# A fused attention and feed-forward kernel: the first matrix product by seven products of quarter blocks in place of eight

## Chip, core and metric

One core of a Trainium2 chip runs the whole kernel. The metric is the device time of one execution in microseconds. The engines are TensorE (PE, matrix products into PSUM), VectorE (DVE), ScalarE (ACT), GpSimd (POOL) and SyncE (SP), which here issues DMA transfers. PSUM has eight banks of 128 x 512 fp32.

## What is computed

```python
def phi(x):                                  # batch 8, heads 8, 576 tokens, 64 wide
    proj = x @ w_phi                         # 64 x 128
    proj = proj - max(abs(proj), axis=-1)
    return concatenate([exp(proj), exp(-proj)])
q_p, k_p = phi(q), phi(k)
kv, z = k_p.T @ v, sum(k_p)
x = (q_p @ kv) / (q_p @ z + 1e-6)            # 4608 tokens x 512
h = x @ w_in                                 # 512 x 2048
g = h * erf(softplus(h))
out = g @ w_out                              # 2048 x 512
```

All is fp32; the weights come as pairs of 32-bit words (they are doubles on the host). The kernel keeps fp32 accuracy in the two large products by splitting each operand into a high and a low fp16 half and adding three products: high x high, high x low, low x high.

## The kernel before

The class `Plan` (line 108) is a list scheduler written into the kernel. Every operation is entered with its engine, a cost in ns, what it reads and writes, and a place in the wanted order (`plan.pos` plus an offset). `Plan.run` (184) then walks through a planned time: at each step it takes the engine that can start earliest and on it the ready operation with the smallest place. A reader on TensorE is held back by `SLACK` ns behind its data. Where the plan sees TensorE without work for over 600 ns it puts filler matmuls on the tile `hot` (1026, called "fillers" below). The result is one fixed order per engine; at run time each engine goes through its order and waits on semaphores.

Attention goes through 72 groups of four tiles of 128 tokens (two heads at a time, a "pair"; four pairs make a batch entry). For each group `project` (517) makes the projections of q and k on TensorE, `front` (485 to 496) takes the maximum and subtracts it on VectorE, `k_piece` makes the exponentials on ScalarE, `t_piece` turns q's part (by TensorE for pairs below `PE_TURNED`, line 568, by a DMA transpose with two VectorE copies, 582 to 585, for the others), `kv_piece` and `n_tile` multiply (helper `columns`, line 401), and `normalise` (644 on) divides. Pairs below `HALVED` are projected in fp32, the others in fp16 halves, made by `halve` (507, 510). The divided tile goes to `xf`, is split into fp16 halves in `xt` (660 to 665), and `x_piece` (700 on) transposes it by DMA into x's tile.

The feed-forward part works on 18 blocks of 256 tokens, each in two halves of eight 128-column groups of w_in. `h_chunk` (803) makes two groups into one PSUM bank: per group, four slices of the 512 inputs by three products, each a pair of matmuls of 64 output rows and 256 columns (helper `mm`, line 391). ScalarE reads each bank out once (822). `erf_gate` (838) applies softplus, erf and the product, and splits the result into `gh` and `gl` (857, 858). `o_chunk` (886) multiplies these by w_out, three products of 512 columns each. All of w_in and w_out stands in SBUF as fp16 halves (`wih`, `wil`, `woh`, `wol`); `load_weight` (423) loads a piece of double words, builds fp32 from the bits in three VectorE steps (440 to 444), and splits it on ScalarE and VectorE (448).

The order of the work is: attention of the first batch entry, then feed-forward halves, with the rest of attention spread between them at a rate set by `BATCH_NS`, and a last stage of feed-forward alone.

Of the kernel before, what the change touches and what calls it, by code (L numbers as in the profile page):

```python
# [8 lines left out]
F32 = mybir.dt.float32  # L9
# [14 lines left out]
TB = 256  # L24
NBLK = NT // TB
GF = 8
NG = 2 * NBLK
HW = GF * TB // 2

SW_PHI = 16.0  # L30
SX = 256.0
SWI = 256.0
# [3 lines left out]
BATCH_NS = 25000.0  # L36
LEAD = 1.05
EARLY = 2 * NPAIR
PE_TURNED = 8
SPEED = {}  # L40
STAY2 = 9000.0
N1 = 7
TWO = 24
ATTN = 5
PH = 2
REST = 4
# [3 lines left out]
X_POOL = 0, 12  # L50
HL_POOL = 8, 16
LATE = 1500.0
FIRST = 4
GAP = 2
XS = 6
N0 = 6
W_EARLY = 7
# [4 lines left out]
BIASED = 0, 9  # L62
KV_ACT = 1, 8
XT_ACT = 0, 12
WRS = 3
GATE_OFF = 4000.0, 4500.0, 5500.0
W_FROM = 12
W_EACH = 7
W_MM = 14
W_OFF = 4000.0  # L70
# [5 lines left out]
STAY = 2500.0  # L76
HALVED = 2 * NPAIR
# [226 lines left out]
def favor_attention_moe(ctx: ExitStack, tc: tile.TileContext, qk, vp, wphi, w_in, w_out, out):  # L304
# [17 lines left out]
    plan.kind("ph", "bank", (("ph",), PH))  # L322
    plan.kind("po", "bank", (("po",), 2))
    plan.kind("pk", "bank", (("pk",), 1))
    plan.kind("pj", "bank", (ATT, 3), (("pj",), 3))
    plan.kind("pj2", "bank", (ATT, ATTN), (("pj2",), ATTN))
    plan.kind("nd", "bank", (ATT, 3), (("nd",), 2))
    plan.kind("nd2", "bank", (ATT, ATTN), (("nd2",), 2))
    plan.kind("p0", "bank", (("p0", "ph", "po", "pk", "pj", "nd"), 7))
# [8 lines left out]
    slots("big", 18, [P, HW], F32)  # L338
    plan.kind("x", "big", (("x",), XS))
    pd = ctx.enter_context(tc.tile_pool(name="pd", bufs=1, space=bass.MemoryType.DRAM))  # L340
    for i in range(2 * FIRST):
        plan.slot("part", f"part{i}", pd.tile([P, DM], F32, tag=f"part{i}", name=f"part{i}"))
    plan.kind("part", "part")
    plan.kind("hs", "big", (("hs",), 4))
    plan.kind("L", "big", (("L",), 4))
    plan.kind("wr", "big", (("wr",), WRS))
    slots("half", 4, [P, 512], F32)
    plan.kind("wf", "half", (("wf",), 2))
    plan.kind("osb", "half", (("osb",), 4))
    plan.kind("acc", "half", (("acc",), 2))  # L350
    whole("gh", 4, [P, HW], F16)
# [16 lines left out]
    whole("xf", 2, [P, 256], F32)  # L368
    whole("xt", 2, [P, 5, 4 * P], F16)
# [5 lines left out]
    const = {k: buf(k) for k in ("ident", "wphi", "w1", "w2", "wih", "wil", "woh", "wol")}  # L375
# [3 lines left out]
    wih, wil, woh, wol = (const[k] for k in ("wih", "wil", "woh", "wol"))  # L379
# [6 lines left out]
    def mm(cost, get, r, w, start, stop):  # L386
        def fn():
            o, a, b = get()
            for i in range(2):
                half = slice(i * D, (i + 1) * D)  # L390
                nc.tensor.matmul(o[half], a[:, half], b, start=start, stop=stop)  # L391

        return op(PE, cost, fn, r=r, w=w, done=cost + 201, mode=COLS)
# [19 lines left out]
    wq = [*range(8), *range(16, 24), *range(8, 16), *range(24, 32)]  # L413
    loaded = set()

    def want(i):
        while i not in loaded:
            load_weight()

    def load_weight():  # L420
        i = wq.pop(0)
        loaded.add(i)
        if i < 16:
            q, c = divmod(i, 4)
            cols = slice(q * 512, (q + 1) * 512)
            src = w_in[c * P : (c + 1) * P, 2 * cols.start : 2 * cols.stop]
            hi, lo, key, s = wih, wil, (c, q), SWI
            at = (slice(None), c, cols)
        else:
            j = i - 16  # L430
            src = w_out[j * P : (j + 1) * P, :]
            hi, lo, key, s = woh, wol, j, SWO
            at = (slice(None), j, slice(None))
        st, f = buf("wr"), buf("wf")
        at_pos = plan.pos
        plan.pos += W_OFF
        word = lambda k: st.t.bitcast(I32).rearrange("p (e w) -> p e w", w=2)[:, :, k]
        q, eng = (POOL, nc.gpsimd) if W_POOL[0] <= i < W_POOL[1] else (SP, nc.sync)
# [187 lines left out]
    def n_tile(qp, t, p, T):  # L626
# [3 lines left out]
        if T == 0:  # L630
            nds[p] = ([buf(kind)], buf("dn"))
            if r == 0:
                xt[p // 2] = buf("xt")
# [452 lines left out]
```

## Time and profile before

| | |
|---|---|
| time, median of 3 runs | 989.9 us (989.17 to 993.82) |
| the profiled execution: span from the first to the last instruction | 989.7 us |
| TensorE matmul busy | 979.3 us, 99% |
| VectorE busy | 626.2 us, 63% |
| ScalarE busy | 673.1 us, 68% |
| GpSimd busy | 48.1 us, 5% |
| moved by DMA | 85.94 MB |
| granted TensorE clock | 0.998 |

The profile has one time for the profiled execution, its span. A "record" is one instruction in the trace; L391 is line 391 of the kernel, often that of a helper, so groups are told apart by their tiles (`bank<-big,wih` is a product of x's tile with w_in's high half). A row of the waits reads: engine, what it writes and line, the engine that released it; total us, times, longest. Busy times of TensorE overlap from one matmul to the next, so the spacing of starts says more than the length of a record.

### The profile page before, as it was taken

Reading aid. Unit: us, or ns where it says so; the run is one execution under the profiler, and the core shown is the slowest. Engines: PE = TensorE matmul, PEld = TensorE weight load, DVE = VectorE, ACT = ScalarE, POOL = GpSimd, SP = SyncE. Lnnn points to the kernel's source line nnn. Section 1 sums busy time; section 2 is a strip of 40 time slices with the busy share of each in tenths; the row PEclk is TensorE's granted clock in tenths of the full one; section 3 lists DMA queues with packets and bytes.
Section 4 is the critical chain, followed back from the end, with each engine's and each line's share of the span. In section 5 each row is a group of like instructions: output and inputs, shape, how many; then the busy total and the mean of one; then the engine's idle time right before and its main releaser. Section 6 shows DMA issues by size and latency. Waiting matters only on the chain.

```text
span 989.7 us, 36415 instructions
## 1 busy us (share of the span) xinstructions
PE 979.3 (99%) x16774; PEld 789.6 (80%) x16774; DVE 626.2 (63%) x1140; ACT 673.1 (68%) x943; POOL 48.1 (5%) x58
## 2 busy tenths in 40 slices
PE   9999998999999999999999999999999999999998
PEld 7897697788878778878878877788888877777776
DVE  6999988898488726666546873587847732123322
ACT  7869859877577756677666757576866645566571
POOL 0201421211000000000000000000000000000000
PEclk9999999999999999999999999999999999999999
DMA  8483692744345502132422722044412310000001
GB/s 311 143 265 97 160 235 76 179 124 101 121 95 107 115 13 55 53 85 50 104 57 43 139 58 60 24 120 95 96 33 51 56 36 12 13 24 2 23 13 33
DMA packets 117385, 85.94 MB, mean 87 GB/s; under 512 B 97904, under 2 KB 98288, under 8 KB 117232
## 3 DMA queue, kind: packets, MB, share of 16 engines
q1 hardware_dynamic: 117088, 83.48, 33.6%
q8 instruction: 131, 2.15, 0.9%
q14 instruction: 22, 0.18, 0.1%
q10 hardware_dynamic: 144, 0.13, 0.0%
HBM read 48.46 MB, written 11.53 MB: 61 GB/s over the span
## 4 chain that ended last, share of the span: by engine, by line
PE 89%; DVE 5%; ACT 5%; issue 1%; DMA 1%; DVEq 0%
PE bank L391 69%; PE bank L401 13%; PE bank L537 5%; PE bank L568 1%; DVE m L485 1%; ACT big L409 1%; ACT big L833 1%; PE bank L1029 1%; DMA part<-half 1%; ACT L850 1%; ACT L833 1%; DVE big L496 0%; DVE big L854 0%; ACT big L822 0%; ACT big L850 0%
## 5 line engine op out<-in xcount | busy, mean ns | idle before, releaser
L391 PE MATMUL bank<-big,wih 128*64 128x256 f16 x4608 | 392.9, 273 | 0.5 <-DVE big L496 0.3
L391 PE MATMUL bank<-big,wil 128*64 128x256 f16 x2304 | 322.2, 273 | 0.2 <-issue 0.2
L391 PEld LDWEIGHTS <-wih 128*64 128x64 f16 x4608 | 260.3, 110 | 26.9 <-issue 1.5
L391 PE MATMUL bank<-woh,gh 128*64 128x512 f16 (+1 forms) x1184 | 224.9, 374 | 0.5 <-DVE big L496 0.5
L391 PE MATMUL bank<-wol,gh 128*64 128x512 f16 (+1 forms) x1184 | 225.3, 374 | 0.0
L391 PE MATMUL bank<-woh,gl 128*64 128x512 f16 (+1 forms) x1184 | 224.9, 374 | 0.0
L822 ACT ACTIVATE big<-bank 128x512 f32<-128x512 f32 x144 | 85.2, 593 | 195.9 <-PE bank L391 195.6
L391 PEld LDWEIGHTS <-gh 128*64 128x64 f16 x2368 | 135.9, 110 | 81.8 <-issue 1.5
L409 ACT ACTIVATE big<-big 128x512 f32<-128x512 f32 x234 | 145.0, 628 | 55.2 <-DVE big L585 27.8
L854 DVE TENSOR_TENSOR big<-big,big 128x1024 f32<-128x1024 f32 x72 | 85.5, 1218 | 144.8 <-ACT big L850 144.6
L391 PEld LDWEIGHTS <-wil 128*64 128x64 f16 x2304 | 134.8, 110 | 1.2 <-issue 0.8
L391 PEld LDWEIGHTS <-gl 128*64 128x64 f16 x1184 | 68.8, 110 | 52.7 <-DVE dn L640 0.2
L485 DVE TENSOR_REDUCE m<-bank 128x4 f32<-128x512 f32 x144 | 92.5, 681 | 25.6 <-PE bank L537 25.4
L858 DVE TENSOR_TENSOR gl<-big,gh 128x1024 f16<-128x1024 f32 x72 | 88.3, 1230 | 27.2 <-ACT gh L857 27.1
L401 PEld LDWEIGHTS bank<-v,big 128*64 128x64 f32 x2016 | 75.9, 138 | 7.5 <-ACT big L409 1.2
L401 PE MATMUL bank<-kv,big 128*64 128x65 f32 x2304 | 81.2, 222 | 0.0
L401 PE MATMUL bank<-v,big 128*64 128x65 f32 (+1 forms) x2016 | 79.8, 228 | 0.6 <-ACT big L409 0.6
L401 PEld LDWEIGHTS bank<-kv,big 128*64 128x64 f32 x2304 | 75.8, 138 | 2.7 <-issue 0.3
L857 ACT CAST gh<-big 128x1024 f16<-128x1024 f32 x72 | 74.2, 1038 | 0.2
L833 ACT ACTIVATE big<-big 128x1024 f32<-128x1024 f32 x72 | 72.5, 1050 | 0.4
L585 DVE COPY big<-plt 128x1024 uint16<-128x1024 uint16 x54 | 42.0, 781 | 43.1 <-DMA plt<-pl 42.9
L925 DVE TENSOR_SCALAR half<-bank 128x512 f32<-128x512 f32 x27 | 18.5, 686 | 59.4 <-PE bank L391 59.4
(55 smaller groups left out, 903.3 us busy)
## 6 DMA issues: line engine op xcount, KB each, us to landing
ld<-in_qk_dram SPq DMA_DIRECT2D x31, 576.0 KB, 4.6
v<-in_vp_dram SPq DMA_DIRECT2D x28, 325.0 KB, 3.3
big<-in_moe_w_in_dram SPq DMA_DIRECT2D x16, 512.0 KB, 5.9
big<-in_moe_w_out_dram SPq DMA_DIRECT2D x16, 512.0 KB, 5.1
out_dram<-half SPq DMA_DIRECT2D x31, 256.0 KB, 2.2
part<-half SPq DMA_DIRECT2D x8, 256.0 KB, 3.7
half<-part SPq DMA_DIRECT2D x8, 256.0 KB, 3.1
big<-in_vp_dram SPq DMA_DIRECT2D x4, 325.0 KB, 7.0
```

What stands on the lines that cost most here:

```text
L391: nc.tensor.matmul(o[half], a[:, half], b, start=start, stop=stop)
L401: nc.tensor.matmul(o[half], a[:, half], b, start=first and c == 0, stop=last and c == 1)
L409: nc.scalar.activation(out_(), in_(), func, **k)
L485: op(DVE, 600, lambda: nc.vector.tensor_reduce(m.t, ps(), axis=AX.X, op=ALU.max, apply_absolute_value=True), r=[b], w=[m])
L537: nc.tensor.matmul(both[nm].t[:, t * P : (t + 1) * P], x()[rows], w.t[rows, :], start=i == 0, stop=i == len(terms) - 1)
L585: op(DVE, 640, lambda: nc.vector.tensor_copy(qview(qp)[:, 1, :].bitcast(U16).rearrange("p (n h) -> p h n", h=2), turned.t.rearrange("p (h ...
L822: o = op(ACT, 490, lambda: nc.scalar.activation(h.t[:, q * 512 : (q + 1) * 512], b.t, AF.Copy, scale=SG / (SX * SWI)), r=[b], w=[(h, q)])
L833: fn = lambda: nc.scalar.activation(L.t, h.t, AF.Softplus, scale=1.0 / SG)
L854: op(DVE, 1140, lambda h=h, L=L: nc.vector.tensor_tensor(h.t, h.t, L.t, op=ALU.mult), r=[L, h], w=[h], port=True, off=GATE_OFF[0] * (v + 1))
L857: op(ACT, 940, lambda h=h, a=a: nc.scalar.copy(a.t, h.t), r=[h], w=[a], off=GATE_OFF[1] * (v + 1))
L858: op(DVE, 1140, lambda h=h, a=a, b=b: nc.vector.tensor_tensor(b.t, h.t, a.t, op=ALU.subtract), r=[h, a], w=[b], port=True, off=GATE_OFF[2] ...
L925: op(DVE, 600, lambda: nc.vector.tensor_scalar_mul(s.t, b.t, scale), r=[b], w=[s])
```

## The change

x times w_in is computed by a scheme with seven products and fifteen additions for a 2 x 2 product of blocks. x is taken in nine "super blocks" of 512 tokens: its blocks are 256 tokens by 256 inputs. w_in is taken in four units of 512 columns: its blocks are 256 inputs by 256 columns. So a unit has seven products of (256 x 256) by (256 x 256) where it had eight, each of 12 pairs of matmuls of 256 columns.

- The sums of blocks of x (S1 to S4) are made in fp32 on VectorE (`combine`), all seven forms are split into fp16 halves (`split`) and transposed by DMA. For the first two super blocks they also go to device memory and come back for a second round.
- The sums of blocks of w_in (T1 to T4) and the fp16 halves of seven forms are made in `split_weights`. Unit 0 stays in SBUF (`RES` = 1). Units 1 to 3 are written to device memory, and `fetch` reads them back, 1.8 MB, for each super block.
- The sums of products are partly made in PSUM: the bank `ha` takes products 1, 6, 5 and 3 one onto the other and is read out by ScalarE after the first, the second, the third and the fourth (`snap`); products 7 and 4 go to `he`, product 2 to `hf`, and VectorE adds these to the tile read out (`add`).
- `o_piece` works per round of two units, so every output tile is made in two rounds and its partial sum goes through device memory.
- Tokens 513 to 576 of the batch entries are gathered in device memory (`tails`) into the ninth super block.
- Constants of the planner are others: pairs 8 and 9 are turned by TensorE too, pairs 8 to 11 are projected in fp32, and the biased form of the exponential goes to group 17.

```diff
-PE_TURNED = 8
+PE_TURNED = 10
-HALVED = 2 * NPAIR
+HALVED = 12
+RES = 1
+WS = 8
+T_POOL = 4
-    whole("wih", 1, [P, NCC, DFF], F16)
-    whole("wil", 1, [P, NCC, DFF], F16)
+    for u in range(RES):
+        whole(f"wi{u}", 1, [P, FORMS, 2, 2, Q], F16)
+    plan.kind("ws", "big", (("ws",), WS))
+    plan.kind("ha", "bank", (HK, HB), (("ha",), 2), ALL)
+    plan.kind("he", "bank", (HK, HB), (("he",), 1), ALL)
+    plan.kind("hf", "bank", (HK, HB), (("hf",), 1), ALL)
+    def fetch(u):
+        wforms[u] = []
+        for i in range(4):
+            b, d = buf("ws"), wstored[u][i]
...
+            op(SP, 430, lambda b=b, d=d, n=n: nc.sync.dma_start(b.t[:, :n], d.t[:, :n]), r=[d], w=[(b, (f, j)) for f in keys for j in range(2)], done=2500, land=1300 * len(keys) * LAND, off=-W_AHEAD)
+    def split_weights(u, j):
...
+        pool = u < T_POOL
+        eng = nc.gpsimd if pool else nc.vector
+        tt = lambda o, oc, x, xc, y, yc, r: op(POOL if pool else DVE, 750 if pool else 330, lambda: eng.tensor_tensor(o.t[:, oc], x.t[:, xc], y.t[:, yc], op=ALU.subtract), r=r, w=[(o, oc.start)], port=True)
+        tt(s, lo, a, hi, a, lo, [a])
+        tt(s, hi, b, hi, a, hi, [a, b])
+        tt(t, lo, b, hi, s, lo, [b, (s, 0)])
+        tt(t, hi, b, lo, t, lo, [b, (t, 0)])
+        for f, x, c, key in ((B11, a, lo, a), (T3, s, hi, (s, Q)), (B21, b, lo, b), (T2, t, lo, (t, 0)), (T1, s, lo, (s, 0)), (B22, b, hi, b), (T4, t, hi, (t, Q))):
...
+            eng = nc.gpsimd if pool else nc.vector
+    def product(n, xf, wf, kind, fresh):
+        s, u = n
+        if fresh:
+            banks[n, kind] = buf(kind)
...
+        for k in range(2):
+            for j in range(2):
+                reads, view = wreads(u, wf, j)
+                for i, (w, lo) in enumerate(((0, 0), (0, 1), (1, 0))):
+                    head = fresh and k == 0 and j == 0 and i == 0
+                    mm(109, lambda k=k, j=j, w=w, lo=lo, view=view: (
+    def snap(n, kind, t, c):
+        b, h = banks[n, kind], hs[n, t]
+        return act(490, lambda: h.t[:, c * 512 : c * 512 + 512], lambda: b.t, AF.Copy, [b], [(h, c)], scale=HSCALE)
+    def add(n, kind, t, c):
...
+        def p1():
+            yield from product(n, A11, B11, "ha", True)
+            first_evac[n] = snap(n, "ha", 0, 0)
+        def p7():
+            yield from product(n, S3, T3, "he", True)
+        def p6():
+            yield from product(n, S2, T2, "ha", False)
+            snap(n, "ha", 1, 0)
+        def p2():
+            yield from product(n, A12, B21, "hf", True)
+            add(n, "hf", 0, 0)
+        def p5():
+            yield from product(n, S1, T1, "ha", False)
+            snap(n, "ha", 1, 1)
+            add(n, "he", 1, 1)
+        def p3():
+            yield from product(n, S4, B22, "ha", False)
+            snap(n, "ha", 0, 1)
+        def p4():
+            yield from product(n, A22, T4, "he", False)
+            add(n, "he", 1, 0)
```

The function `tt` in `split_weights` looks up `eng` only when the order is written out, and by then the loop below it has set `eng` again.

Three places in the orders follow. First VectorE, among the first 60 of its rows, in the attention of the first batch entry while the first weights come in; L485 and L581 are the maxima, L496 and L592 the subtractions, L448 the low half of a weight piece, L530 the low half of a weight form, L520 the difference of weight blocks. Before:

```order
L442 SCALAR_TENSOR_TENSOR half1_106<-big13_90,half1_106 128x512
L642 RECIPROCAL dn0_140<-dn0_140 128x4
L444 SCALAR_TENSOR_TENSOR half1_106<-big13_90,half1_106 128x512
L485 TENSOR_REDUCE m0_122<-bank4_65 128x4
L485 TENSOR_REDUCE m1_123<-bank1_62 128x4
L488 TENSOR_SCALAR mb2_130<-m0_122 128x4
L657 TENSOR_TENSOR xf0_142<-bank3_64,dn0_140 128x256
L448 SCALAR_TENSOR_TENSOR wil0_74<-half0_105,wih0_73 128x512
L496 TENSOR_TENSOR uq0_132<-bank1_62,m1_123 128x512
```

And now:

```order
L480 SCALAR_TENSOR_TENSOR half10_152<-big13_89,half10_152 128x512
L530 SCALAR_TENSOR_TENSOR wi00_73<-half0_142,wi00_73 128x256
L482 SCALAR_TENSOR_TENSOR half10_152<-big13_89,half10_152 128x512
L530 SCALAR_TENSOR_TENSOR wi00_73<-half11_153,wi00_73 128x256
L520 TENSOR_TENSOR half11_153<-half10_152,half0_142 128x256
L581 TENSOR_REDUCE m0_177<-bank4_65 128x4
L581 TENSOR_REDUCE m1_178<-bank1_62 128x4
L520 TENSOR_TENSOR half12_154<-half10_152,half11_153 128x256
L592 TENSOR_TENSOR uq0_187<-bank1_62,m1_178 128x512
L520 TENSOR_TENSOR half12_154<-half10_152,half12_154 128x256
```

Between the same maxima and subtractions of attention there now stand four rows of forms and differences of 256 columns where one low half of 512 stood, and the differences are VectorE's.

Second TensorE, late, in a feed-forward step without attention; shown is the first row in each bank, and the dots are the rows that go on in it. Before, where a bank's 24 pairs of h are followed by products with w_out (`woh`) and by another bank:

```order
L391 MATMUL bank0_61<-big13_90,wih0_73 64x256
...
L391 MATMUL bank5_66<-woh0_75,gh1_110 64x512
...
L391 MATMUL bank2_63<-big13_90,wih0_73 64x256
...
L391 MATMUL bank1_62<-big13_90,wih0_73 64x256
...
L391 MATMUL bank6_67<-big13_90,wih0_73 64x256
...
L391 MATMUL bank3_64<-woh0_75,gh2_111 64x512
```

And now, from product 1 of unit 0 of the ninth super block (`wi0` is unit 0's resident form):

```order
L424 MATMUL bank7_68<-half17_159,wi00_73 64x256
...
L424 MATMUL bank5_66<-half0_142,wi00_73 64x256
...
L424 MATMUL bank0_61<-half12_154,wi00_73 64x256
...
L424 MATMUL bank1_62<-woh0_74,gh0_164 64x512
...
L424 MATMUL bank7_68<-half11_153,wi00_73 64x256
```

Before, each bank holds one result and the next products go to another. Now the sum bank (bank7 here) is written again after two products in other banks, 24 matmuls each, and four matmuls with w_out; a product is read from another tile of x (`half17`, `half0`, `half12`, `half11`) each time.

Third SyncE's queue, late in the mixed part; L471 is a piece of a weight unit from device memory, L1072 a partial sum on its way back, L1076 a store of the output, L680 a transpose of q, L554 and L558 loads of attention's inputs. Before (L584 is the transpose of q, L721 that of x, L928 the store):

```order
L928 DMA out_0_dram<-half0_105 128x512
L584 DMA_TRANSPOSE plt0_136<-pl0_134 128x8x128
L462 DMA v0_120<-in_vp_dram 128x650
L584 DMA_TRANSPOSE plt1_137<-pl1_135 128x8x128
L458 DMA ld2_119<-in_qk_dram 128x1152
L928 DMA out_0_dram<-half2_107 128x512
L721 DMA_TRANSPOSE big7_84<-xt0_144 128x8x128
L721 DMA_TRANSPOSE big10_87<-xt0_144 128x8x128
```

And now:

```order
L1072 DMA half15_157<-part11_109 128x512
L680 DMA_TRANSPOSE plt1_192<-pl1_190 128x8x128
L680 DMA_TRANSPOSE plt0_191<-pl0_189 128x8x128
L471 DMA big6_82<-wd2_114 128x1024
L1076 DMA out_0_dram<-half2_144 128x512
L471 DMA big14_90<-wd3_115 128x1024
L558 DMA v1_176<-in_vp_dram 128x650
L471 DMA big17_93<-wd4_116 128x1024
L471 DMA big4_80<-wd5_117 128x512
```

The four pieces of a unit stand in the queue one by one between the other issues; the whole queue has 503 issues where it had 256.

More of the change, by code (lines that the diff above doesn't have):

```diff
@@ L374, in favor_attention_moe @@
     hot = sb.tile([P, 512], F16, tag="hot", name="hot")
-    const = {k: buf(k) for k in ("ident", "wphi", "w1", "w2", "wih", "wil", "woh", "wol")}
+    const = {k: buf(k) for k in ("ident", "wphi", "w1", "w2", *(f"wi{u}" for u in range(RES)), "woh", "wol")}
     for b in const.values():
@@ L418, in want, with wform @@
+    def want(item):
+        while item not in loaded:
             load_weight()
[L420 to L436, printed above, removed]
+    def wform(u, f):
+        if u < RES:
+            b = const[f"wi{u}"]
+            return b, f, lambda hl, j: b.t[:, f, hl, j, :]
+        b = wforms[u][f // 2]
+        return b, f, lambda hl, j: b.t.bitcast(F16).rearrange("p (f h j n) -> p f h j n", f=2, h=2, j=2)[:, f % 2, hl, j, :]
@@ L948, in moe_step @@
     def moe_step(h, o):
[L949 to L963 removed]
+        prods = h_unit(h) if h else []
```

560 lines of the change are left out of this document (320 added, 240 removed).

## The prediction

> **What bounds the kernel now.** I read the page's table of engines first, then TensorE's (PE's) waits, then the stretches, then single rows of the timeline.
>
> ```profile
> span 989.7 us, 36415 instructions
> PE 979.3 (99%) x16774; PEld 789.6 (80%) x16774; DVE 626.2 (63%) x1140; ACT 673.1 (68%) x943; POOL 48.1 (5%) x58
> ```
> ```profile
> PE bank L537 <- DVE big L496: 3.6, 1, 3.6
> PE bank L1029 <- DVE hot L1035: 1.4, 1, 1.4
> PE bank L391 <- DVE big L496: 0.9, 2, 0.5
> ```
> ```profile
> 0.00:50.00 50.00, 48.55 (x946) 41.16 (x948) 41.45 (x99) 40.67 (x120) 8.12 (x18) 1.00 0.65 225
> 50.00:100.00 50.00, 49.78 (x924) 42.77 (x920) 48.04 (x92) 41.01 (x64) 5.09 (x6) 1.00 0.59 184
> 100.00:150.00 50.00, 49.27 (x954) 40.24 (x950) 44.39 (x84) 35.06 (x65) 16.13 (x16) 1.00 0.80 190
> 150.00:200.00 50.00, 46.43 (x846) 38.44 (x842) 41.77 (x73) 46.02 (x64) 10.34 (x10) 0.97 0.56 141
> 200.00:250.00 50.00, 49.14 (x873) 41.39 (x870) 45.06 (x70) 37.77 (x55) 8.42 (x8) 1.00 0.39 109
> 500.00:600.00 100.00, 100.00 (x1770) 80.11 (x1766) 66.97 (x133) 67.23 (x85) 0.00 (x0) 1.00 0.41 85
> 800.00:900.00 100.00, 100.00 (x1392) 76.63 (x1388) 26.64 (x24) 59.54 (x64) 0.00 (x0) 1.00 0.04 15
> ```
> Columns after the length: busy PE, weight load, DVE, ACT, POOL, then granted clock, DMA share, GB/s. TensorE never stands still for long: 6 us of waits in the three largest rows, one of them 3.6 us. A busy TensorE could still be a slow one, so I looked at starts:
>
> ```profile
> 799.74 0.39 PE L391 MATMUL bank<-big,wih 128*64 128x256 f16 x4
> 799.96 0.28 PE L391 MATMUL bank<-big,wil 128*64 128x256 f16 x2
> ...
> 801.38 0.38 PE L391 MATMUL bank<-woh,gh 128*64 128x512 f16 x2
> ...
> 803.97 0.39 PE L391 MATMUL bank<-big,wih 128*64 128x256 f16 x4
> ```
> From 799.74 to 801.38 stand 15 pairs of 256 columns: 0.109 us a pair. From 801.38 to 803.97 stand 12 pairs of 512: 0.216 us. They follow each other without a hole, so a pair taken away is its 0.109 us won, as long as nothing else becomes late. VectorE (DVE) is the one to fear: 48.04 of 50 us busy from 50 to 100 us, but 27 of 100 at the end. The first 250 us are a stage with two near bounds, the rest belongs to TensorE.
>
> **The change part by part.** The sum is made against the profiled span of 989.7 us; the runs' median is 989.9, so I take them as the same.
>
> *Products.* Before, x times w_in is 3456 pairs of 256 columns (6912 records). Now it is 9 x 4 x 7 x 12 = 3024. 432 pairs x 0.109 = **-47.1 us**, all on the bound. The second multiplication keeps its columns.
>
> *Attention on TensorE.*
> ```profile
> 23.93 1.16 PE L537 MATMUL bank<-wphi,ld 64*128 64x128 f32 x16
> 25.02 0.84 PE L1029 MATMUL bank<-hot 128*64 128x512 f16 x6
> ...
> 29.95 0.66 PE L568 MATMUL bank<-ident,uq 128*128 128x128 f32 x4
> 30.54 0.66 PE L401 MATMUL bank<-big,big 128*64 128x130 f32 x8
> ```
> ```profile
> 530.95 1.45 PE bank L537 x48
> 532.40 9.13 PE bank L391 x128
> ```
> HALVED moves nine groups of four tiles from fp16 projections (1.45 / 2 = 0.725 us) to fp32 ones (25.02 - 23.93 = 1.09): 9 x 0.365 = **+3.3**. PE_TURNED adds five groups of transposes on TensorE at 30.54 - 29.95 = 0.59: **+2.9**. The order holds 90 filler matmuls for 46: 22 pairs x 0.216 = **+4.8**; they may lie in time that TensorE would wait anyway, so 0 to 4.8, and I take all.
>
> *Switches between kinds of tile.*
> ```profile
> 105.39 0.38 PE L391 MATMUL bank<-wol,gh 128*64 128x512 f16 x2
> 105.70 0.84 PE L537 MATMUL bank<-w,ld 64*128 64x128 f16 x24
> 106.47 0.41 PE L391 MATMUL bank<-woh,gl 128*64 128x512 f16 x2
> ```
> A projection block alone takes 106.47 - 105.39 - 0.216 = 0.86 us where half a double one takes 0.725: 0.14 for going in and out. The new order has 172 changes of kind for 132, 20 more visits: **+2.8** (0 if they fall into waits).
>
> *VectorE early.* This decides the rest.
> ```profile
> 148.52 0.67 DVE L496 TENSOR_TENSOR uq<-bank,m 128x512 f32<-128x512 f32 x1
> 149.12 0.68 DVE L448 SCALAR_TENSOR_TENSOR wil<-half,wih 128x512 f16<-128x512 f32 x1
> 149.71 0.68 DVE L582 COPY pl<-uq 128x1024 uint16<-128x1024 uint16 x1
> 150.32 0.75 DVE L440 TENSOR_SCALAR half<-big 128x512 int32<-128x512 int32 x2
> ```
> ```profile
> L858 DVE TENSOR_TENSOR gl<-big,gh 128x1024 f16<-128x1024 f32 x72 | 88.3, 1230 | 27.2 <-ACT gh L857 27.1
> L665 DVE TENSOR_TENSOR xt<-xf,xt 128x256 f16<-128x256 f32 x40 | 16.6, 414 | 0.3
> L919 DVE SCALAR_TENSOR_TENSOR half<-bank,half 128x512 f32<-128x512 f32 x8 | 5.4, 680 | 6.8 <-PE bank L391 6.8
> ```
> Rows of 0.68 us start 0.60 apart, so I price each by its mean less 0.08: 0.60 for 512 elements, 1.14 for 1024, 0.335 for 256. New are 108 additions out of PSUM (65 us), the splits and combinations of x (49 x about 0.34, 42 and 36 x 0.60, for 60 casts and 60 differences less: about +35), 56 low halves and 32 differences of the weight forms (29.5, for 16 x 0.60 less) and 29 more partial sums (17). The weight differences stand in VectorE's order although the code names GpSimd. Together about +130 us.
>
> The tightest place in the order is TensorE's row that reads the seventh L1034 result. Ahead of that result VectorE has 424 rows: 54 maxima and 36 subtractions (54), 25 weight rows in three steps (38.5), the 88 quarter-size rows (29.5), 14 additions (8.4), 15 gate rows (17), 22 normalisations (7.5), 9 combinations (5.4) and some 20 us of small ones: 181 us. TensorE has ahead of it 432 pairs of 256 (47.1), 124 of 512 (26.8), 27 fp32 groups and one fp16 (30.1), 23 transposed groups (13.5), 45 fillers (9.7) and 1664 records of L401 at 0.029 and some longer (51): 178 us. So both have the same work there, where before TensorE was ahead in work. In before TensorE reaches such a point some 14 us later than such prices say (start 1.4, first matmuls at half clock 2, some 80 changes of kind at 0.07, waits 5). VectorE may lose as little as 13.5 us (8.5 in the first 50, then 4% as from 50 to 100) or 24 (its idle time in the first 200 us). It is done at 194 to 205, TensorE asks at 192: late by 2 to 13 us. I take **+6**, nearer the lower end, because the row nearest to a VectorE that is the bound is the stretch with 4% idle; end to end 0 to 13, below nothing not, as work there only grows.
>
> A wait has a second price:
> ```profile
> 160.41 0.85 PE L537 MATMUL bank<-w,ld 64*128 64x128 f16 x24 [3.57 <-DVE big L496]
> ...
> 162.26 0.64 PE L391 MATMUL bank<-woh,gh 128*64 128x512 f16 x2
> 162.68 0.63 PE L391 MATMUL bank<-wol,gh 128*64 128x512 f16 x2
> ```
> After the 3.57 us wait a pair of 512 takes 0.42 us, and the stretch's clock is 0.97: 1.5 us of 50 lost. I take the 6 us as several shorter waits, with 0 for this; one such wait would add 1.5. The Trainium skill, "TensorE: Matmul & The Clock Gate", HAM oscillation, says that TensorE falls to half clock after gaps above about 3.4 us; the one gap here agrees. By that rule two such gaps would make the sum 3 us longer.
>
> *Behind cover.* ScalarE's 55 more rows, most of 256 or 128 columns and some 10 us net, lie beside TensorE (41 of 50 us busy at most early, 67 of 100 later). VectorE from 500 to 600 us goes from 67% to about 80%. Weight forms come back 27 times, 1.84 MB each, 49.5 MB; the first stretch moves 225 GB/s at a share of 0.65, so 346 at full: 143 us, 15% more of a DMA that the stretches show at 0.04 to 0.80. SP has twice the rows. If this cover fails, see the third rival. The tail stays: one VectorE row and two stores.
>
> Sum: 989.7 - 47.1 + 3.3 + 2.9 + 4.8 + 2.8 + 6 = **962.4**, forecast **962 us**. Its own range: without the VectorE wait, the switches and the fillers 949; with 13 for VectorE and two falls of the clock 972.
>
> **The rivals.**
>
> *VectorE paces the whole first stage.* Its next close reading has 225 us of work ahead, TensorE 228. If VectorE also keeps its idle time of before, 29 us in 250 (50 less each busy time), that comes out at 254 against TensorE's 242; with each wait feeding the next (maximum, subtraction, exponential, then TensorE) I allow twice this, 12 to 25 us in place of 6: 968 to 981. For it: 48.04 of 50. Against: that idle time was spent mostly waiting for TensorE.
>
> *One PSUM bank carries four products.* The sum bank of a unit is read out by ScalarE three times and added to again, 108 times in all.
> ```profile
> L822 ACT ACTIVATE big<-bank 128x512 f32<-128x512 f32 x144 | 85.2, 593 | 195.9 <-PE bank L391 195.6
> ```
> If TensorE stood for each 0.593 us read-out, 64 us: 956 + 64 = 1020, slower. It decides from 34 / 108 = 0.31 us a time. Against it: in the order at least 14 pairs of 512 (3 us) or two products lie between two uses. The Trainium skill, "Perfetto Trace Analysis", Matmuls, advises to rotate independent groups through different banks so that a read-out overlaps the next group; no row of before shows a bank used in this other way.
>
> *Weights come late.*
> ```profile
> big<-in_moe_w_out_dram SPq DMA_DIRECT2D x16, 512.0 KB, 5.1
> ```
> A form tile of 512 KB takes 5.1 us to land. If SP, with 500 issues in one line, sends a fetch only when its unit begins, 27 x 5.1 = 138 us and the time is 1100; behind a fetch that waits stand the transposes of x and the partial sums. It decides from 27.5 / 27 = 1.0 us per fetch. Against it: eight buffers hold two units, so a fetch can go one unit (some 25 us) ahead, and the order mixes it among other issues.
>
> *The columns are saved and nothing else changes:* no VectorE wait, fillers in idle time: 951. It lies in the forecast's range.
>
> **How the numbers follow.** Forecast 0.74 (with the last case), VectorE's stage 0.16, bank 0.05, weights 0.05. Low end 950, high end 979: below and above lie the two slow rivals and a little of the first. A measurement here can tell about 0.5% (5 us) from no change. Below 985: the forecast and nearly all of the VectorE rival, 0.88; within, 0.04 (a bank or weight case of part size); slower 0.08.
>
> **What would show it.** The count of 256-column records falls from 6912 to 6048 with 0.109 a pair kept; if the pair is longer, the first term is wrong. TensorE's waits before 250 us should be on VectorE (subtractions, additions, low halves) and sum to 5 to 15 us; nearly none after 300 us. The clock there 0.97 or more. Waits on ACT's read-outs of the sum bank, or on DMA into the form buffers, above 10 us would prove the second or third rival. VectorE busy near 770 us in all (its 626 and some 140 by whole means). If the time is above 985, the early stage or the fetches were misjudged.

## The result and the profile after

The changed kernel takes 968.37 us (median of 4 runs, 968.24 to 969.21) where the kernel before takes 991.86 on the same chip (4 runs, 989.17 to 995.14): a ratio of 0.9758, 95% interval 0.9733 to 0.9784. The profiled execution has a span of 966.5 us for 989.7. 23.2 us are won; the forecast was 962, with 950 to 979 as its range. The time lies 1.8 us above the span here (968.28 and 966.5 in the profiled execution). The prediction took the two as the same, so its sum, made in spans, is to be held against 966.5.

The table of engines of the changed kernel:

```profile
PE 947.7 (98%) x15806; PEld 754.5 (78%) x15806; DVE 752.7 (78%) x1351; ACT 681.9 (71%) x1000; POOL 43.9 (5%) x35
```

TensorE is busy 31.6 us less, VectorE 126.5 us more. The stretches show where TensorE pays for that (columns as in the prediction: busy PE, weight load, DVE, ACT, POOL, granted clock, DMA share, GB/s):

```profile
0.00:50.00 50.00, 48.55 (x932) 40.98 (x932) 41.23 (x110) 39.81 (x124) 2.98 (x8) 1.00 0.70 226
50.00:100.00 50.00, 45.45 (x879) 38.76 (x879) 49.59 (x120) 38.07 (x106) 9.48 (x7) 1.00 0.97 264
100.00:150.00 50.00, 45.92 (x770) 37.35 (x768) 48.21 (x93) 40.89 (x63) 5.81 (x5) 1.00 0.94 277
150.00:200.00 50.00, 47.32 (x818) 38.44 (x814) 49.86 (x104) 42.27 (x67) 10.27 (x5) 1.00 0.82 267
200.00:250.00 50.00, 48.82 (x798) 38.09 (x796) 49.58 (x80) 40.46 (x56) 9.38 (x7) 1.00 1.03 294
...
500.00:600.00 100.00, 99.90 (x1734) 78.44 (x1731) 79.95 (x138) 70.54 (x91) 0.00 (x0) 1.00 0.62 157
```

From 50 to 250 us VectorE is busy 197 of 200 us, and TensorE stands still 12.5 us of them (200 less its four busy times). From 500 to 600 us VectorE has a fifth of its time left and TensorE none. TensorE's waits of the changed kernel, the first seven:

```profile
PE bank L424 <- DVE big L964: 3.0, 3, 1.6
PE bank L424 <- ACT gh L1033: 2.3, 2, 2.0
PE bank L633 <- DVE kv L710: 1.8, 2, 1.1
PE bank L424 <- ACT big L442: 1.5, 3, 0.9
PE bank L1178 <- DVE hot L1184: 1.4, 1, 1.4
PE bank L633 <- DVE big L754: 1.3, 2, 0.9
PE bank L424 <- DVE gl L1034: 1.2, 1, 1.2
```

The waits are many and short, on VectorE's additions (L964), copies (L710), divided tiles (L754) and low halves (L1034), and on ScalarE's rows that VectorE feeds. None is on a DMA. The groups of TensorE and VectorE that the change is about:

```profile
L424 PE MATMUL bank<-half,big 128*64 128x256 f16 x4536 | 274.1, 273 | 3.4 <-DVE big L964 2.3 <-ACT big L442 1.1
...
L424 PE MATMUL bank<-half,wi 128*64 128x256 f16 x1512 | 93.3, 273 | 1.2 <-DVE big L964 0.7 <-ACT big L442 0.4
```
```profile
L964 DVE SCALAR_TENSOR_TENSOR big<-bank,big 128x512 f32<-128x512 f32 x108 | 73.9, 686 | 71.6 <-PE bank L424 67.0 <-ACT big L442 4.6
```

The first two are 6048 records of 256 columns together, as the change says. The third are the 108 additions.

### The profile page after: what moved, and what is told of

The parts are those of the page before. It is cut to its first block, busy times and chain, and to the rows that moved or that the text cites. A ratio compares the mean times of both kernels' runs of the same rounds, so it can differ in the third digit from the quotient of the medians.

```text
span 966.5 us, 35295 instructions
## 1 busy us (share of the span) xinstructions
PE 947.7 (98%) x15806; PEld 754.5 (78%) x15806; DVE 752.7 (78%) x1351; ACT 681.9 (71%) x1000; POOL 43.9 (5%) x35
## 3 DMA queue, kind: packets, MB, share of 16 engines
q8 instruction: 123, 2.02, 0.9%
## 4 chain that ended last, share of the span: by engine, by line
PE 78%; DVE 3%; issue 0%; DVEq 0%
PE bank L424 65%; PE bank L434 9%; PE bank L633 4%; DVE gl L1034 0%; DVE m L581 0%; DVE half L482 0%; DVE big L530 0%; DVE big L592 0%; DVE half L480 0%; DVE big L964 0%; DVE half L520 0%; DVE big L1030 0%; DVE uq L592 0%; DVE big L754 0%; DVE half L478 0%
## 5 line engine op out<-in xcount | busy, mean ns | idle before, releaser
L424 PE MATMUL bank<-half,big 128*64 128x256 f16 x4536 | 274.1, 273 | 3.4 <-DVE big L964 2.3
L424 PEld LDWEIGHTS <-big 128*64 128x64 f16 x4536 | 247.7, 110 | 22.8 <-issue 4.5
L442 ACT ACTIVATE big<-bank 128x512 f32<-128x512 f32 x190 | 111.1, 603 | 143.7 <-PE bank L424 140.5
L424 PE MATMUL bank<-woh,gh 128*64 128x512 f16 x1024 | 199.1, 380 | 2.3 <-ACT gh L1033 2.3
L424 PE MATMUL bank<-woh,gl 128*64 128x512 f16 x1024 | 198.6, 380 | 1.2 <-DVE gl L1034 1.2
L424 PE MATMUL bank<-wol,gh 128*64 128x512 f16 x1024 | 198.9, 379 | 0.0
L442 ACT ACTIVATE big<-big 128x512 f32<-128x512 f32 x206 | 127.6, 628 | 71.0 <-DVE big L592 35.0
L424 PEld LDWEIGHTS <-gh 128*64 128x64 f16 x2048 | 119.2, 110 | 74.7 <-ACT gh L1033 2.9
L964 DVE SCALAR_TENSOR_TENSOR big<-bank,big 128x512 f32<-128x512 f32 x108 | 73.9, 686 | 71.6 <-PE bank L424 67.0
L581 DVE TENSOR_REDUCE m<-bank 128x4 f32<-128x512 f32 x144 | 92.7, 684 | 21.7 <-PE bank L633 21.5
L424 PEld LDWEIGHTS <-gl 128*64 128x64 f16 x1024 | 61.3, 110 | 45.9 <-DVE gl L1034 1.7
L424 PE MATMUL bank<-half,wi 128*64 128x256 f16 x1512 | 93.3, 273 | 1.2 <-DVE big L964 0.7
L1034 DVE TENSOR_TENSOR gl<-big,gh 128x1024 f16<-128x1024 f32 x64 | 80.4, 1265 | 13.5 <-ACT gh L1033 13.5
L424 PEld LDWEIGHTS <-wi 128*64 128x64 f16 x1512 | 81.4, 110 | 6.3 <-issue 1.9
L592 DVE TENSOR_TENSOR uq<-bank,m 128x512 f32<-128x512 f32 x72 | 49.2, 683 | 0.6 <-PE bank L664 0.5
```

Of the source, the lines that this page charges most:

```text
L442: nc.scalar.activation(out_(), in_(), func, **k)
L581: op(DVE, 600, lambda: nc.vector.tensor_reduce(m.t, ps(), axis=AX.X, op=ALU.max, apply_absolute_value=True), r=[b], w=[m])
L592: op(DVE, 600, lambda: nc.vector.tensor_tensor(to(), ps(), m.t.unsqueeze(2).to_broadcast([P, GT, NF]), op=ALU.subtract), r=[b, m], w=[key])
L964: op(DVE, 640, lambda: nc.vector.scalar_tensor_tensor(h.t[:, c * 512 : c * 512 + 512], b.t, HSCALE, h.t[:, c * 512 : c * 512 + 512], op0=A ...
L1034: op(DVE, 1140, lambda h=h, a=a, b=b: nc.vector.tensor_tensor(halfs(b), h.t, halfs(a), op=ALU.subtract), r=[h, a], w=[b], port=True, off=G ...
```

## The experiments

The theory: the saved columns are won in full, and a part is given back in the first 250 us, where VectorE cannot keep up. Its rivals: the constants and the new order make the gain and not the columns; or what is given back is something else, fillers, fetches or VectorE's load throughout. All times are beside the changed kernel, which was run again with the first of them. The runs come from three groups, on different chips, and the base ran in the first alone, beside the runs with the differences on GpSimd, no fillers and two constants back. The kernel before ran in each, with medians of 992.63, 993.07 and 992.22 us, so a difference below 1 us between groups says nothing.

**The changed kernel again.**

> The changed kernel once more, as the base for the others. Both theories: a span of 966.5 us within 0.5 us, a time of 968 to 969 us.

968.45 us (5 runs, 968.29 to 968.78), ratio to the kernel before 0.9758 [0.9734, 0.9782], span 967.0. This is the base below. One row says how its first 300 us go, and such a row stands with most of the experiments:

```profile
0.00:300.00 300.00, 286.42 (x4974) 230.94 (x4976) 277.47 (x559) 235.61 (x454) 44.44 (x35) 0.99 0.85 247
```

TensorE is idle 13.58 us there. In the kernel before it is 6.83:

```profile
0.00:300.00 300.00, 293.17 (x5416) 245.53 (x5418) 255.01 (x481) 233.84 (x407) 48.10 (x58) 0.99 0.58 159
```

**More VectorE work early.** Theory: VectorE sets TensorE's pace up to 250 us and nowhere later. Rival: it is merely full, and the order has slack.

```diff
-lambda: eng.tensor_tensor(o.t[:, oc], x.t[:, xc], y.t[:, yc], op=ALU.subtract)
+lambda: [eng.tensor_tensor(o.t[:, oc], x.t[:, xc], y.t[:, yc], op=ALU.subtract) for _ in range(2)]
```

> Each of the 32 differences of weight halves (L520, 256 columns, 0.335 us each end to end) is done twice on VectorE, with the same result: 10.7 us more of VectorE, all before 200 us, and not one instruction more for TensorE. Theory (VectorE sets the pace up to 250 us: its busy share there is 97 to 99 per cent): 972 to 979, 4 to 10.7 us over the changed kernel's 968.4; the TensorE waits on VectorE before 250 us grow by as much. Rival (VectorE is merely full, TensorE's order has slack, so that 10 us more are hidden): within 1.5 us of 968.4.

982.26 us (4 runs, 981.10 to 983.11), ratio 0.9891 [0.9856, 0.9925]. Its first 300 us:

```profile
0.00:300.00 300.00, 276.67 (x4756) 223.27 (x4758) 280.68 (x576) 231.61 (x445) 43.14 (x34) 0.99 0.83 242
```

10.7 us of VectorE by my price (12.0 by its busy time over the whole run, 765.6 for 753.6) cost 13.8 us. TensorE is idle 23.33 us, 9.8 more, and its clock fell in two stretches of 50 us (0.97 each) in place of one. There was no slack, and a little more than the theory's upper end was lost.

**The same load later.** For this edit the operation in `add` becomes a function of two instructions.

```diff
             h.t[:, c * 512 : c * 512 + 512], b.t, HSCALE, h.t[:, c * 512 : c * 512 + 512], op0=ALU.mult, op1=ALU.add)
+        if 4 <= n[0] < 7:
+            nc.vector.tensor_tensor(hot[:, 0:256], h.t[:, c * 512 : c * 512 + 256], h.t[:, c * 512 + 256 : c * 512 + 512], op=ALU.subtract)
```

> The same kind of load, put later: 36 more VectorE subtractions of 256 columns (some 12 us) behind the additions of super blocks 4 to 6, into an unused tile. Theory (VectorE matters in the first 250 us only): 967 to 970, so within 1.5 us of the changed kernel's 968.4, though VectorE is over 80 per cent busy there. Rival (the changed kernel is near VectorE's bound throughout): 974 to 980.

969.27 us (4 runs, 969.05 to 971.45), ratio 0.9762 [0.9732, 0.9792], 0.8 us over the base. The added group of VectorE, with first and last start, and the stretch that it lies in, first of this run and then of the base:

```profile
L968 DVE TENSOR_TENSOR hot<-big x36: 424/425/427, 496.5 to 785.7; 128x256 f16<-128x256 f32 x36
```
```profile
300.00:950.00 650.00, 649.26 (x10720) 502.52 (x10718) 487.87 (x825) 446.16 (x547) 0.00 (x0) 1.00 0.56 146
```
```profile
300.00:950.00 650.00, 649.66 (x10722) 515.78 (x10720) 473.50 (x790) 446.25 (x547) 0.00 (x0) 1.00 0.57 146
```

14.4 us more of VectorE and 0.4 us more of idle TensorE: VectorE's bound ends with the first stage. (VectorE is 75% busy in this stretch, not over 80% as I had expected.)

**No fillers.** The sum had 4.8 us for 22 more filler pairs.

```diff
-                        order.append((at, -1, lambda s=spare[0]: filler(self.slots[s])))
```

> The 31 pairs of filler matmuls inside the order are left out (the seven pairs ahead of all work and the six at 6.6 us belong to them only in part: the first seven stay). Theory as in the prediction's sum (each filler pair costs its 0.216 us): 38 pairs x 0.216 = 8.2 us less, span 958 us. Rival (the fillers stand where TensorE would wait for VectorE or ScalarE anyway): no change within 1 us, and slower by 1 to 2 us if a gap lets the clock fall.

973.09 us (4 runs, 970.26 to 974.50), ratio 0.9802 [0.9775, 0.9829], span 968.5. First 300 us:

```profile
0.00:300.00 300.00, 278.93 (x4878) 226.61 (x4880) 275.79 (x556) 234.77 (x452) 42.76 (x35) 0.99 0.85 247
```

38 filler pairs are gone (8.2 us by 0.216), and the idle time is 7.5 us longer. The fillers cost nothing; they lie in time in which TensorE would wait. My term was wrong. The median rises by 4.6 us and this span only by 1.5 because the profiled execution was the fastest of the four. It has a granted clock of 0.998; the other three have 0.995 to 0.996 and spans of 971.0 to 972.7. All five of the base have 0.998 or 0.999. A clock that is 0.2 to 0.3% lower over 970 us is 2 to 3 us, most of the difference. So without the fillers the clock fell more in three of four executions.

**The differences really on GpSimd.** `tt` looks up `eng` too late, so the 32 differences are VectorE's. Here they are GpSimd's:

```diff
+        t_eng, t_pool = eng, pool
-        tt = lambda ...: op(POOL if pool else DVE, ..., lambda: eng.tensor_tensor(...
+        tt = lambda ...: op(POOL if t_pool else DVE, ..., lambda: t_eng.tensor_tensor(...
```

> The 32 differences of weight blocks really run on GpSimd, where the code names it, instead of on VectorE; nothing else moves. Theory (VectorE paces the first 250 us, 97% busy from 20 to 250 us): VectorE loses 32 x 0.335 = 10.7 us of work before its tightest place, so the roughly 8 us that TensorE waits there more than before go down by 4 to 8 us: span 958.5 to 962.5 us. Rival (the early delay is order and latency, not VectorE's work): no change within 1 us, or slower, since GpSimd is slower per row.

966.73 us (4 runs, 964.03 to 968.29), ratio 0.9738 [0.9711, 0.9766]; span 963.7, 3.3 less. In time the two cannot be told apart, and the span falls short of the 958.5 to 962.5 expected. VectorE's busy time over the whole run falls by 6.0 us only (747.6 for 753.6), though 32 more rows of this kind had added 12.0. Other rows must have become longer. VectorE's rows in the base, with 44.4 us of GpSimd work:

```profile
L592 DVE TENSOR_TENSOR uq<-bank,m 128x512 f32<-128x512 f32 x72 | 49.1, 682 | 0.6 <-PE bank L664 0.5
...
L530 DVE SCALAR_TENSOR_TENSOR big<-half,big 128x256 f16<-128x256 f32 x42 | 16.4, 439 | 0.0
```

And in this run, with 71.1 us of GpSimd work (all lines from 520 on are one higher):

```profile
L593 DVE TENSOR_TENSOR uq<-bank,m 128x512 f32<-128x512 f32 x72 | 49.1, 682 | 1.1 <-PE bank L665 0.5
...
L531 DVE SCALAR_TENSOR_TENSOR big<-half,big 128x256 f16<-128x256 f32 x42 | 20.3, 528 | 0.4 <-ACT big L442 0.4
```

A row that reads PSUM keeps its 682 ns; a row that reads two tiles of SBUF goes from 439 to 528. The 42 rows alone give back 3.7 us. The Trainium skill, "SBUF — State Buffer", Who interferes with whom, says that a VectorE instruction with two SBUF inputs contends with a GpSimd instruction that reads SBUF, and that one with at most one SBUF input does not, outside the two-port modes; these two rows agree.

**GpSimd's load by itself.** Is it GpSimd's work that slows them, or the other order?

```diff
+    extra = sb.tile([P, 256], F32, tag="extra", name="extra")
-        op(POOL if pool else DVE, ..., lambda: eng.tensor_tensor(tv(1), view(), tv(0), op=ALU.subtract), ...)
+        op(POOL if pool else DVE, ..., lambda: [eng.tensor_tensor(tv(1), view(), tv(0), op=ALU.subtract)] + ([nc.gpsimd.tensor_tensor(extra, extra, extra, op=ALU.mult) for _ in range(2)] if pool else []), ...)
```

The halvings of q and k get the same two.

> GpSimd's load measured by itself: behind each of its 29 rows stand two more multiplications of 256 columns in a tile that nobody reads (58 x 0.73 = 42 us of GpSimd before 270 us), and nothing else changes; the plan and the order of all other engines are the same. Theory (GpSimd's work slows VectorE's rows, by some 7 us per 27 us in the run with the differences there): 973 to 981. Rival (GpSimd's load is free, it is idle most of that time): within 1.5 us of 968.4.

976.43 us (5 runs, 975.59 to 978.66), ratio 0.9838 [0.9814, 0.9861]. Its first 300 us:

```profile
0.00:300.00 300.00, 281.10 (x4846) 229.24 (x4848) 285.15 (x552) 233.16 (x449) 94.72 (x94) 0.99 0.85 244
```

50 us of GpSimd work that nobody reads cost 8.0 us. Over the whole run VectorE has not one row more than in the base, but is busy 11.2 us longer. First the base, then this run:

```profile
PE 948.6 (98%) x15806; PEld 754.6 (78%) x15806; DVE 753.6 (78%) x1351; ACT 681.9 (71%) x1000; POOL 44.4 (5%) x35
PE 950.5 (98%) x15806; PEld 758.3 (78%) x15806; DVE 764.8 (78%) x1351; ACT 682.0 (70%) x1000; POOL 95.1 (10%) x94
```

TensorE is idle 5.3 us longer before 300 us. Its waits there on VectorE's additions grew from 2.2 to 5.6 us and those on the divided tiles from 0.9 to 2.7; none is on GpSimd or on a DMA. That GpSimd's load slows VectorE is shown. Not only rows with two SBUF inputs are slower: the copy of q's part (`pl<-uq`, one SBUF input) goes from 699 to 741 ns in the mean.

**More to GpSimd, with the plan's knowledge.**

```diff
-X_POOL = 0, 3
+X_POOL = 0, 5
-HL_POOL = 8, 16
+HL_POOL = 8, 24
```

The edit of `tt` above is in it too.

> More than the weight differences goes from VectorE to GpSimd, and the plan knows it: the 32 differences, 16 more halvings of q and k (pairs 16 to 23) and 14 more low halves of x (super blocks 3 and 4). VectorE is spared 10.7 us of differences and some 10 us of halvings. Theory A (every microsecond that VectorE is spared before 250 us counts, up to TensorE's waits there of some 12 us): 954 to 961. Theory B (VectorE's rows become slower while GpSimd works, as with the differences alone on GpSimd, where L530 rose from 418 to 483 ns and 10.7 us spared gave 3.3): 963 to 969.

967.26 us (4 runs, 966.06 to 968.21), ratio 0.9743 [0.9720, 0.9765]. Theory B: the same group in this run,

```profile
L531 DVE SCALAR_TENSOR_TENSOR big<-half,big 128x256 f16<-128x256 f32 x42 | 21.5, 556 | 0.0
```

is slower again. This and the run with the differences on GpSimd have the shortest times here, but neither can be told from the changed kernel by its interval.

**Two planner constants back.**

```diff
-PE_TURNED = 10
+PE_TURNED = 8
-HALVED = 12
+HALVED = 8
```

> Pairs 8 to 11 are projected from fp16 halves and pairs 8 and 9 turned by DMA, as before. By the prediction's prices TensorE loses 3.3 + 2.9 = 6.2 us of work; VectorE gains five turns of two copies (6.2 us of work). Theory (VectorE is the bound early): the 6.2 us of TensorE are not won there, and the copies come on top: slower by 2 to 8 us, span 968 to 975. Rival (TensorE is the bound all through): 960 us.

990.01 us (12 runs, 987.68 to 993.78), ratio 0.9977 [0.9961, 0.9994]. 21.6 us are lost, nearly all that the change wins, though TensorE has 6.2 us less to do, fillers aside. First 300 us:

```profile
0.00:300.00 300.00, 276.09 (x4798) 223.92 (x4800) 276.05 (x547) 227.38 (x444) 54.08 (x43) 0.98 0.86 246
```

TensorE is idle 10.3 us longer, and the order holds 196 filler records for 90. Neither theory had that size, so each constant ran alone.

**HALVED alone.**

```diff
-HALVED = 12
+HALVED = 8
```

> Of the two constants that cost 20 us together when set back, HALVED alone goes from 12 to 8: four more pairs of tiles are split into fp16 halves (8 subtractions more on GpSimd, 8 casts more on ScalarE), nine groups of projections go from fp32 to fp16 (3.3 us less of TensorE), and the planned order holds 77 fillers in place of 45. VectorE's number of rows stays. Theory A (the 20 us come from the VectorE rows that PE_TURNED brings): within 3 us of 968.4. Theory B (they come from the projections that wait for GpSimd's halves, and from the order that goes with them): 976 to 985.

984.99 us (4 runs, 983.41 to 986.52), ratio 0.9915 [0.9884, 0.9946]: 16.5 us lost.

```profile
0.00:300.00 300.00, 276.14 (x4842) 224.97 (x4842) 272.99 (x542) 231.20 (x447) 57.02 (x43) 0.99 0.85 244
```

**PE_TURNED alone.**

```diff
-PE_TURNED = 10
+PE_TURNED = 8
```

> The other constant alone: PE_TURNED from 10 to 8. Five groups of four tiles are turned by DMA and not by TensorE: 2.9 us less of TensorE, ten VectorE rows more (five of 0.6 and five of 0.5 to 0.7, some 6 us) in its full stage, five more DMA transposes. Theory A (VectorE's early work is what counts): 974 to 985, most of the 20 us that both constants cost together. Theory B (it is HALVED's work): within 4 us of 968.4.

977.16 us (4 runs, 976.38 to 977.55), ratio 0.9836 [0.9807, 0.9864]: 8.7 us lost.

```profile
0.00:300.00 300.00, 285.02 (x4894) 231.81 (x4896) 277.43 (x560) 233.56 (x449) 42.84 (x35) 0.99 0.88 249
```

Both matter, HALVED more (theory B of its own run; of PE_TURNED's, the range of theory A, though 8.7 us are not most of the 20), and 16.5 + 8.7 is more than the 21.6 of both. With HALVED at 8 VectorE has no row more (1351), yet over the whole run it is busy 7.1 us longer (760.7 for 753.6), and TensorE is idle 10.3 us longer before 300 us. GpSimd has 12.6 us more work, and VectorE's group of 42 low halves,

```profile
L530 DVE SCALAR_TENSOR_TENSOR big<-half,big 128x256 f16<-128x256 f32 x42 | 19.8, 518 | 0.1
```

takes 518 ns a row in place of 439, some 3.3 us. That agrees with GpSimd's work slowing VectorE, but does not part it from the rest: the plan also makes another order, and both constants also set the pace of attention (line 1141): with HALVED at 8 the third batch entry gets 1.9 us less of planned time, with PE_TURNED at 8 it gets 4.0 less. How much comes from each was not taken apart. With PE_TURNED at 8 little idle time is added, but 40 more filler pairs (170 filler records for 90), and the stretch from 100 to 150 us has a clock of 0.93, with one long wait in it:

```profile
PE bank L424 <- DVE uq L592: 3.9, 1, 3.9
```

The change sets more constants than these two (`BATCH_NS` from 25000 to 23000, `STAY` from 2500 to 1500 and others). No run sets those back, and none gives the kernel before the new ones, so what the constants would be worth without the scheme is open.

**Eight products again.**

```diff
             yield from product(n, A11, B11, "ha", True)
+            yield from product(n, A11, B11, "ha", True, False)
```

The new last argument keeps the bank of the first pass.

> Eight products per unit again, with all else as changed: the first product of every unit is done a second time over itself (its first pass opens the bank anew, so the result stays). 12 x 36 = 432 pairs of 256 columns more. Theory (a column of TensorE is worth 0.109 us a pair, but in the first 250 us some of it lies where TensorE waits for VectorE): 1004 to 1016 from 968.4, that is 36 to 47 more. Rival (the gain came from the new constants and order, not from the columns): under 990.

1037.89 us (4 runs, 1036.12 to 1038.81), ratio 1.0453 [1.0428, 1.0477]: 69.4 us more, above the theory's upper end. The order holds 160 filler records for 90, TensorE's first 300 us are

```profile
0.00:300.00 300.00, 280.05 (x4926) 229.16 (x4928) 278.99 (x568) 224.78 (x444) 41.77 (x35) 0.99 0.84 242
```

and two stretches of 50 us have a clock of 0.97. The rival is out: the columns are worth their 47.1 us, and more goes with them, since every longer unit also shifts the plan.

**Each fetch twice.**

```diff
-lambda ...: nc.sync.dma_start(b.t[:, :n], d.t[:, :n])
+lambda ...: [nc.sync.dma_start(b.t[:, :n], d.t[:, :n]) for _ in range(2)]
```

> Each of the weight forms that come back from device memory is fetched twice into the same buffer: 49.5 MB more through the DMA queues (the profile's 170.82 MB become some 220) and as many issues more on SyncE. Theory (fetches lie a unit ahead and behind TensorE's work): 967 to 972. The third rival of the prediction (weights come late): 980 or more, with TensorE waits on the form buffers.

1143.11 us (6 runs, 1135.78 to 1148.34), ratio 1.1503 [1.1463, 1.1543], 174.7 us more. My expectation missed what the edit does: the second transfer writes the buffer of the first, so its issue waits on SyncE's queue for the landing. The largest of SyncE's waits, and a piece of the chain of work that ended last:

```profile
SPq L471 <- DMA big<-wd: 446.4, 108, 7.9
```
```profile
258.04 4.52 DMA big<-wd
...
270.38 7.32 DMA plt<-pl
```

108 issues wait 4.1 us each, and behind them stand the transposes of q and x and with them VectorE, ScalarE and TensorE. TensorE is idle 126 us more than in the base and busy 41 us longer, at a granted clock of 0.941. So the run measures a held queue, with the clock that falls in its waits, and not the load: 174.7 / 108 = 1.6 us per held issue, 6.5 per fetch. Whether 49.5 MB more alone would cost anything was not tried.

**The account.** For eight of the runs: the span over the base's 967.0, and what it is made of. Work is the terms of the prediction (0.109 a pair, 3.3 and 2.9 for the constants), fillers count 0.216 a pair, idle is taken from the rows of 300 us, and the clock is (1 - granted clock) x 50 us over the stretches of 50, each over the base.

| run | span | work | fillers | idle | clock | sum |
|---|---|---|---|---|---|---|
| differences on GpSimd | -3.3 | 0 | 0 | -1.4 | -1.5 | -2.9 |
| differences twice | +12.3 | 0 | 0 | +9.8 | +1.5 | +11.3 |
| no fillers | +1.5 | 0 | -8.2 | +7.5 | 0 | -0.7 |
| GpSimd's load | +7.7 | 0 | 0 | +5.3 | 0 | +5.3 |
| both constants | +20.5 | -6.2 | +11.4 | +10.3 | +3.5 | +19.0 |
| HALVED 8 | +16.0 | -3.3 | +6.9 | +10.3 | 0 | +13.9 |
| PE_TURNED 8 | +7.6 | -2.9 | +8.6 | +1.4 | +2.0 | +9.1 |
| eight products | +67.3 | +47.1 | +7.6 | +9.1 | +1.5 | +65.3 |

(Eight products: 6.4 of the idle time before 300 us, 2.7 behind.) The sums hold within 2.4 us, most of them a little short. So fillers, idle time and clock are one cost in three forms: TensorE waiting in the first stage, for VectorE and for ScalarE's rows beside it (with HALVED at 8, some 4.5 of the 10.3 us are waits on ScalarE).

## Why the prediction came out as it did

**Products, -47.1: right.** 6048 records are left, and in the changed kernel 10 pairs take 1.10 us from one start to the next:

```profile
543.39 1.26 PE L424 MATMUL bank<-half,big 128*64 128x256 f16 x20
544.49 1.33 PE L434 MATMUL bank<-kv,big 128*64 128x65 f32 x40
...
546.30 1.04 PE L424 MATMUL bank<-half,big 128*64 128x256 f16 x16
547.28 0.84 PE L633 MATMUL bank<-w,ld 64*128 64x128 f16 x24
548.05 0.41 PE L424 MATMUL bank<-woh,gh 128*64 128x512 f16 x2
548.29 0.38 PE L424 MATMUL bank<-wol,gh 128*64 128x512 f16 x2
```

**HALVED and PE_TURNED, +3.3 and +2.9: right as TensorE's work, but read as a cost only.** Set back, they cost 16.5 and 8.7 us. In the sum the VectorE term already went by the changed constants, so the sum stood; but the text says nowhere that most of the gain hangs on them. With both set back the kernel is 0.2% faster than the one before, so the saved 47.1 us are won only with a plan that fits.

**Fillers +4.8 and VectorE +6: the sum right, the parts wrong.** Fillers lie in waits (the run without them). What VectorE costs is 13.95 - 6.83 = 7.1 us more of idle TensorE before 300 us and the 4.8 us of fillers that fill the rest of its waits, 11.9 for 10.8. So VectorE was late by twice my 6, near the upper end of 13, and two fifths of it showed as fillers. That the two terms together came out near is luck. The stretch with 4% idle was a poor nearest row: VectorE is busy 96 to 100% from 50 to 250 us.

**Switches, +2.8: too small.** In the rows above a single projection block takes 548.05 - 547.28 = 0.77 us where half a double one takes 0.725, and the pair behind it 0.24 in place of 0.216, which I had left out. The way in is seen here:

```profile
509.88 0.38 PE L424 MATMUL bank<-wol,gh 128*64 128x512 f16 x2
510.20 1.51 PE L633 MATMUL bank<-w,ld 64*128 64x128 f16 x48
```

0.32 - 0.216 = 0.10. That makes 0.17 a visit for my 0.14, so 3.4 us. The Trainium skill, "TensorEngine Tiling (Array Packing)", Key Properties, says that a change of tiling mode drains TensorE; the 0.10 us on the way in agree.

**"The tail stays": wrong by 1.2 us.** Before, the last rows were

```profile
986.53 0.42 DVE L879 TENSOR_SCALAR half<-bank 128x256 f32<-128x256 f32 x1 [0.89 <-PE bank L391]
986.99 0.38 ACTq L884 DMA_DIRECT2D out_dram<-half  x1
```

and now

```profile
962.08 0.69 DVE L1073 SCALAR_TENSOR_TENSOR half<-bank,half 128x512 f32<-128x512 f32 x1 [4.49 <-PE bank L424]
962.80 1.11 SPq L1076 DMA_DIRECT2D out_dram<-half  x2
```

3.2 us from the last VectorE row to the end of the span became 4.4: the row has twice the columns (0.69 us for 0.42), and two stores follow it through SyncE's queue (1.11 us to issue, for 0.38).

**The sum again:** 989.7 - 47.1 + 3.3 + 2.9 + 11.9 + 3.4 + 1.2 - 1.5 (the stretch at clock 0.97 is gone) = 963.8 for a span of 966.5. 2.7 us stay unexplained.

**The rivals.** VectorE's stage: partly true; 11.9 us lie just under its 12 to 25. The bank: TensorE waits 1.5 us in all for L442, the line of ScalarE's read-outs, and no more than 0.9 at once, so they lie behind the other products. The weights: TensorE waits for no DMA, so it is out. The harm of a held queue that it names is real: in the run with each fetch twice a fetch costs 6.5 us, half clock included, and the rival decides from 1.0. Columns alone, 951: out, as VectorE is late.

**What would show it:** VectorE's waits were to sum to 5 to 15 us before 250 us; in the seven rows they are 8.7 (with 1.4 at the start). After 300 us there was to be nearly none, and there is 0.3 us up to 950 in the base. VectorE's busy time was to be near 770 and is 752.7.

## What to carry to other kernels

When a change takes work from the bound engine and gives it to one that is nearly full, price the stage in which that one is full by itself: here each microsecond added to VectorE before 250 us cost 1.3, and after 300 us none. Fillers, idle time and a fallen clock were one loss in three forms here, so count them together. Before moving rows from VectorE to GpSimd, look at what VectorE's other rows read: here 10.7 us taken off VectorE won 3.3 us of span at most, as its rows with two SBUF inputs, and some copies, became slower.

## What was not expected of the hardware

The clock can fall after a short wait. The base and the first profile are the same kernel, and both have one wait of 2.0 us (L424 on ScalarE's `gh`) at 135 us. The stretch around it, first in the base and then in the first profile:

```profile
130.00:140.00 10.00, 7.98 (x76) 4.54 (x74) 9.19 (x15) 8.79 (x11) 0.00 (x0) 0.87 1.02 345
```
```profile
130.00:140.00 10.00, 7.98 (x90) 4.71 (x88) 9.17 (x15) 9.08 (x12) 0.00 (x0) 1.00 0.97 313
```

The same idle 2.02 us left the clock at 1.00 once and took it to 0.87 once. The rule of the Trainium skill in the prediction ("TensorE: Matmul & The Clock Gate", HAM oscillation) speaks of gaps above about 3.4 us; the 3.9 us wait with PE_TURNED at 8 agrees, the 2.0 us one does not, and the measurement decides.

GpSimd seems to be hit by the sharing as well. In the run that moved the differences, the smaller group of them takes 0.73 us a row at the least, but 1.63 in the mean,

```profile
L521 POOL TENSOR_TENSOR half<-half 128x256 f32<-128x256 f32 x8 | 13.0, 1628 | 69.2 <-DVE half L482 47.5 <-issue 21.7
```

and at 161.58 us one took 4.33,

```profile
161.58 4.33 POOL L521 TENSOR_TENSOR half<-half 128x256 f32<-128x256 f32 x1 [5.22 <-DVE half L482]
```

while VectorE went through rows with two SBUF inputs without a pause, up to 165.24 us, where a row that reads PSUM follows:

```profile
161.96 1.22 DVE L1031 TENSOR_TENSOR big<-big,big 128x1024 f32<-128x1024 f32 x1
163.10 1.22 DVE L1035 TENSOR_TENSOR gl<-big,gh 128x1024 f16<-128x1024 f32 x1
164.23 1.09 DVE L531 SCALAR_TENSOR_TENSOR big<-half,big 128x256 f16<-128x256 f32 x3
```

GpSimd's row ends at 165.91, 0.67 us behind that place. This is one row, and no run tests it by itself.
